# Start of a gated linear attention and MLP kernel: the order of constants, and the queue and place of three loads

## The chip, the cores and the metric

The kernel runs on one core of a Trainium2 chip. A core has a matrix engine (TensorE, PE in the profile), a vector engine (VectorE, DVE), an engine for activation functions and copies (ScalarE, ACT), a general engine (GpSimd, POOL) and one that mainly issues transfers (SyncE, SP). They run side by side, each through its own list of instructions in order, and wait for one another on semaphores. Transfers between the large memory (HBM) and the core's own memory (SBUF) are issued by SP or ACT on hardware queues, or by POOL on a software queue, which can also convert types on the way. PSUM is the small memory that TensorE writes to.

The metric is the device time in microseconds, as a median over runs.

## What is computed

The inputs are q, k, v and alpha, each of 4 batches, 8 heads, 768 positions and head size 48, and two weight matrices. Per head a 48 x 48 state decays by alpha and takes in an outer product; the result goes through a two-layer network with a gelu.

```python
for t in range(S):
    state = alpha[:, :, t, :, None] * state + np.einsum('bhd,bhe->bhde', k[:, :, t], v[:, :, t])
    y[:, :, t] = np.einsum('bhd,bhde->bhe', q[:, :, t], state)
# x: y with the heads side by side, 3072 x 384
h = x @ w_in                                       # 384 x 2048
g = 0.5 * h * (1.0 + np.tanh(c * (h + 0.044715 * h * h * h)))
return g @ w_out                                   # 2048 x 384
```

All comes and goes in float32; the kernel works in bfloat16 and float16 inside.

## The kernel before

The sequence is cut into six chunks of 128 positions, and two batches at a time form a pair: twelve pairs, worked through as (chunk 0, batches 0 and 1), (chunk 0, batches 2 and 3), (chunk 1, ...) and so on. They are called pair 0, pair 1, pair 2 below; `j` is the batch within a pair.

For each pair ScalarE takes the logarithm of alpha (L296 or L298), TensorE sums it along the positions with a triangular matrix (L283 and L287, or L315 and L317), and ScalarE forms exp of the sums: `b`, `binv` and `bend` (L332, L338). VectorE multiplies q by `b` and k by `binv` (L349: `qp`, `kp`). TensorE transposes both (L359), ScalarE or VectorE copies the transposes out of PSUM (L377: `qkT`), TensorE forms the scores of a batch (L414: `at`) and VectorE masks them (L421: `atm`). Then `y` is the product of the masked scores with v (L463), plus the state's part from the second chunk on (L460). `y` is copied (L470: `x`), transposed (L477) and copied again (L481: `xT`). The state is carried on with L431 and L448 (for the first pairs after k has been transposed back, L385 and L392).

The network runs in twelve blocks, one a pair: layer 1 in 16 column blocks of three matmuls each (L487: `hT`), a gelu for each (L493), and layer 2 (L501: `acc`). The result is copied (L508) and stored (L513). ScalarE loads its function table anew when it goes from exp and logarithm to gelu or back (L208).

Pairs 0 and 1 are "packed". Their q, k and alpha come in four pieces each, of 32 partitions with 192 values in a run, so that a run is long; the positions of a chunk then lie in another order, and the sums of L283 need special block masks, `ut_blk` and `blk`, in place of the plain triangle.

What is issued in what order on every engine is decided when the program is built. `tasks` makes a list of tasks with costs, dependencies and priorities; `Scheduler.order` goes through it with costs from the table `W` and gives each engine its list. Where it sees TensorE idle for long in the first 60 us by its own plan, it puts in filler matmuls on a tile of zeros (L217), whose results nobody reads. The number of fillers ahead of the first real matmul is the planned idle time divided by `cold`. The orders of the constants and of the loads are not planned; they are written out:

- `run` (from L728) has the constants: `zero`, `ones`, the triangle and the identity (these two in part on POOL), then the zeros in the pads of the ring buffers for `la`, `qp` and `kp` (L738), the zero states (L741), then `blk` and `ut_blk` (L742 to L750), then a bfloat16 copy of the triangle (L751). Except for the two parts on POOL, all of that is VectorE's.
- `RINGS` lists the packed pieces (tensor, pair, piece) and the engine that issues each. SP or ACT issue them from the first instruction on.
- `LOADS` lists what POOL's software queue loads: `v0` is v of pair 0 (converted to bfloat16 on the way), `in 0` a quarter of w_in, `out 0` a quarter of w_out, a bare number all of a later pair. `gatek0` is not a load: POOL copies one column of k of pair 0 into a scratch tile (L250), and so does not go on before that k has landed. A step beginning with `p` loads the four pieces of a packed tensor on POOL's queue; there was none.

POOL's list at the start is therefore: gate on k of pair 0, v of pair 0, gate on q of pair 1, w_in 0, v of pair 1, w_in 1 to 3, w_out 0 and 1, then pair 2. Loads on a queue take eight semaphores in turn, so a load also waits until the one eight places ahead of it has landed.

## Time and profile before

| | |
|---|---|
| median of 5 runs | 188.19 us (187.1 to 189.17) |
| the profiled execution | 186.78 us |
| its span, first to last instruction | 185.0 us |
| PE busy | 174.7 us, 94% |
| ACT busy | 136.2 us, 74% |
| DVE busy | 105.2 us, 57% |
| granted TensorE clock | 1.0 |

The profile is one execution. The page gives each engine's busy time, then the span in 40 slices with the busy share of each in tenths, the transfers, the chain of work that ended last, and the costliest groups of instructions. The trace behind it gives single instructions, what they waited for, and when a transfer landed. Times within the span count from its first instruction. A busy PE counts fillers too: there are 16 of them, 7.9 us in sum.

Some transfers at the start, from the trace:

| load | queue | issued | landed |
|---|---|---|---|
| q, pair 0, four pieces | SP and ACT | 1.66 to 2.16 | 5.00 to 5.80 |
| k, pair 0, four pieces | SP | 3.40 to 4.71 | 6.03 to 7.38 |
| alpha, pair 1, four pieces | SP | 5.20 to 6.61 | 7.70 to 9.37 |
| q, pair 1, four pieces | SP | 7.08 to 8.51 | 9.96 to 11.12 |
| v, pair 0 | POOL | 8.08 | 14.67 |
| k, pair 1, four pieces | SP | 8.98 to 10.44 | 12.53 to 15.03 |
| w_in, part 0 | POOL | 11.73 | 16.62 |
| v, pair 1 | POOL | 12.47 | 18.80 |
| w_in, parts 1, 2, 3 | POOL | 13.66, 14.39, 15.15 | 21.01, 23.21, 25.12 |
| w_out, part 0 | POOL | 15.90 | 27.11 |

### The profile page before, as it was taken

The numbers are of one execution on the slowest core, as the hardware profiler recorded it, in microseconds if no ns is written. First come the engines' busy times: TensorE is split into PE (matmuls) and PEld (weight loads), VectorE is DVE, ScalarE is ACT, GpSimd is POOL, SyncE is SP. The second block draws the span as 40 slices with busy tenths as digits, with TensorE's granted clock in tenths as the row PEclk, the third lists the DMA queues.
The fourth block names the chain that finished last, engine by engine and source line by source line (L and its number), as shares of the span: only waits on it lengthen the run. The fifth ranks groups of instructions, "written<-read, shape, count | busy, mean of one in ns | idle before, by whom it ended". The sixth has DMA issues, their size and how long they took to land.

```text
span 185.0 us, 4590 instructions
## 1 busy us (share of the span) xinstructions
PE 174.7 (94%) x1840; PEld 127.4 (69%) x1842; DVE 105.2 (57%) x235; ACT 136.2 (74%) x308; POOL 58.6 (32%) x64
## 2 busy tenths in 40 slices
PE   7595999999999999999999999999999999999992
PEld 2353779666687787687688769667677677686861
DVE  8576763079677596597499798596644715000000
ACT  3495869865979869859799759788789884491931
POOL 2259545994663566565660200000000000000000
PEclk9999999999999999999999999999999999999999
DMA  5899999999999999999999976054171290311102
GB/s 159 220 175 175 184 211 204 211 226 172 185 276 190 157 234 198 178 231 202 180 216 231 186 198 119 19 130 99 24 168 53 43 200 4 87 43 46 43 0 85
DMA packets 50613, 27.56 MB, mean 149 GB/s; under 512 B 37984, under 2 KB 47712, under 8 KB 50592
## 3 DMA queue, kind: packets, MB, share of 16 engines
q0 software_dynamic: 31904, 17.30, 68.7%
q1 hardware_dynamic: 18112, 9.57, 20.7%
q10 hardware_dynamic: 576, 0.39, 0.7%
q8 instruction: 14, 0.23, 0.6%
q14 instruction: 7, 0.06, 0.1%
HBM read 25.17 MB, written 4.72 MB: 162 GB/s over the span
## 4 chain that ended last, share of the span: by engine, by line
PE 81%; DMA 8%; ACT 4%; DVE 3%; issue 1%; SPq 1%; POOL 0%; POOLq 0%; DVEq 0%
PE acc L501 32%; PE hT L487 31%; PE at L414 4%; DMA v<-in_v_dram 4%; PE qkT_ps L359 3%; PE yps L463 3%; PE yps L460 2%; PE cum L315 2%; PE kv L431 2%; DMA qkT<-kp 2%; PE xT_ps L477 2%; DMA k<-in_k_dram 1%; DMA a<-in_alpha_dram 1%; DVE atm L421 1%; DVE st L448 1%
## 5 line engine op out<-in xcount | busy, mean ns | idle before, releaser
L493 ACT ACTIVATE gT<-hT 128x256 bf16<-128x256 f32 x192 | 63.9, 386 | 10.6 <-PE hT L487 9.9
L487 PE MATMUL hT<-xT,w_in 128*128 128x256 bf16 x576 | 70.5, 273 | 0.3 <-ACT gT L493 0.2
L501 PE MATMUL acc<-w_out,gT 128*128 128x384 bf16 x384 | 68.9, 326 | 0.0
L487 PEld LDWEIGHTS <-w_in 128*128 128x128 bf16 x576 | 54.0, 98 | 8.6 <-DVE xT L481 0.6
L501 PEld LDWEIGHTS <-gT 128*128 128x128 bf16 x384 | 35.6, 97 | 20.3
L421 DVE TENSOR_TENSOR atm<-at,ut 128x512 bf16<-128x512 f32 x48 | 31.1, 686 | 14.5 <-PE at L414 13.8
L349 DVE TENSOR_TENSOR qp<-q,b 128x768 bf16<-128x768 f32 (+1 forms) x15 | 11.8, 793 | 15.4 <-ACT b L338 15.4
L508 ACT COPY ot<-acc 128x384 f32<-128x384 f32 x16 | 7.7, 480 | 14.3 <-PE acc L501 13.3
L230 POOL DMA_DIRECT2D v<-in_v_dram x13 | 14.6, 1123 | 10.3 <-DMA v<-in_v_dram 2.6
L338 ACT ACTIVATE b<-cum 128x768 bf16<-128x768 f32 (+1 forms) x15 | 10.2, 683 | 7.5 <-PE cum L317 2.6
L230 POOL DMA_DIRECT2D k<-in_k_dram x11 | 12.2, 1108 | 10.3 <-DVE kp L349 4.7
L230 POOL DMA_DIRECT2D a<-in_alpha_dram x11 | 12.2, 1113 | 7.0 <-DMA q<-in_q_dram 2.8
L230 POOL DMA_DIRECT2D q<-in_q_dram x11 | 12.2, 1111 | 6.3 <-DMA w_out<-in_moe_w_out_dram 1.1
L208 ACT ACT_TABLE_LOAD x9 | 11.5, 1283 | 2.8 <-issue 2.6
L448 DVE TENSOR_TENSOR st<-stmp,bend 64x192 bf16<-64x192 f32 x32 | 11.3, 353 | 1.6
L349 DVE TENSOR_TENSOR kp<-k,binv 128x768 bf16<-128x768 f32 (+1 forms) x15 | 11.8, 792 | 0.4 <-ACT binv L338 0.2
L446 DVE TENSOR_TENSOR stmp<-kv,st 64x192 f32<-64x192 f32 x32 | 11.3, 352 | 0.9 <-PE kv L431 0.6
L493 ACT ACT_TABLE_LOAD x9 | 11.5, 1283 | 0.2
L470 ACT CAST x<-yps 128x384 bf16<-128x384 f32 x13 | 6.2, 479 | 6.8 <-PE yps L463 6.8
L470 DVE CAST x<-yps 128x384 bf16<-128x384 f32 x11 | 6.1, 556 | 7.7 <-PE yps L463 7.6
L463 PE MATMUL yps<-v,atm 128*128 128x48 bf16 x192 | 8.7, 183 | 1.6 <-DMA v<-in_v_dram 0.9
L338 ACT ACTIVATE binv<-cum 128x768 bf16<-128x768 f32 (+1 forms) x15 | 10.2, 679 | 0.0
(61 smaller groups left out, 161.8 us busy)
## 6 DMA issues: line engine op xcount, KB each, us to landing
out_dram<-ot SPq DMA_DIRECT2D x24, 192.0 KB, 2.7
a<-in_alpha_dram POOLq DMA_DIRECT2D x9, 384.0 KB, 13.1
q<-in_q_dram POOLq DMA_DIRECT2D x9, 384.0 KB, 13.2
k<-in_k_dram POOLq DMA_DIRECT2D x9, 384.0 KB, 13.4
v<-in_v_dram POOLq DMA_DIRECT2D x11, 192.0 KB, 12.9
w_in<-in_moe_w_in_dram POOLq DMA_DIRECT2D x4, 384.0 KB, 8.1
w_out<-in_moe_w_out_dram POOLq DMA_DIRECT2D x4, 384.0 KB, 11.3
k<-in_k_dram SPq DMA_DIRECT2D x8, 96.0 KB, 3.3
```

The costliest lines, as they stand in the source:

```text
L208: nc.scalar.add_instruction(mybir.InstLoadActFuncSet(name=nc.get_next_instruction_name(), act_func_set_id=i, engine=mybir.EngineType.Activ ...
L230: (nc.sync if e == "SP" else nc.gpsimd).dma_start(u[n][:, lo:hi].rearrange("t b h d -> t (b h) d"), src)
L338: self.nc.scalar.activation(u[n].rearrange("t i h d -> t i (h d)")[:, lo:hi], cum, AF.Exp, scale=1.0 if n == "b" else -1.0)
L349: self.nc.vector.tensor_tensor(out, rows, b, op=ALU.mult)
L421: self.nc.vector.tensor_tensor(u["atm", i][:, o], u["at", i][:, o], self.ut[:, None, :].to_broadcast([self.C, self.H // 2, self.C]), op=AL ...
L446: nc.vector.tensor_tensor(s[ps], acc, old[ps, :, fs], op=ALU.add)
L448: nc.vector.tensor_tensor(new[ps, :, fs], acc, u["bend"][ps, i, :, None].to_broadcast([64, H // 2, D]), op=ALU.mult)
L463: nc.tensor.matmul(y[:, h, :], u["atm", i][:, h % 2, h // 2, :], u["v"][:, i, h, :], start=c == 0, stop=True, skip_group_check=True)
L470: self.copy(e)(x, u["y", i].rearrange("t h d -> t (h d)"))
L487: self.nc.tensor.matmul(h, self.w_in[:, j, nt * self.C:(nt + 1) * self.C], self.xT[c][:, j, lo:hi].rearrange("p g t -> p (g t)"), start=j ...
L493: return lambda e: self.nc.scalar.activation(self.gT[c % self.NG][:, nt, lo * self.C:hi * self.C], f.pop(("h", c, lo, nt)), AF.Gelu_apprx_ ...
L501: self.nc.tensor.matmul(f["acc", c, b], self.gT[c % self.NG][:, nt, b * self.C:(b + 1) * self.C], self.w_out[:, nt, :], start=nt == 0, sto ...
```

## The change

In `run`, the zeros in the ring buffers' pads and the zero states move behind the block masks. In `LOADS`, POOL waits for q of pair 0 instead of k of pair 0, and has no second gate; k of pair 1 is loaded by POOL, in the same four pieces, right behind v of pair 0, and its four entries leave SP's list; v of pair 1 comes behind w_in 0 and w_in 1. In the planner's table `cold` goes from 400 to 380.

```diff
-    ... piece=330, piece_issue=450, begin=2700, cast_p=2300, ln_packed=1040, cold=400, fill=216, zero=1100,
+    ... piece=330, piece_issue=450, begin=2700, cast_p=2300, ln_packed=1040, cold=380, fill=216, zero=1100,
...
-    LOADS = ('gatek0', 'v0', 'gateq1', 'in 0', 'v1', 'in 1', 'in 2', 'in 3', 'out 0', 'out 1', '2a', ...)
+    LOADS = ('gateq0', 'v0', 'pk1', 'in 0', 'in 1', 'v1', 'in 2', 'in 3', 'out 0', 'out 1', '2a', ...)
...
-    RINGS = (... ('q', 1, 3, 'SP'), ('k', 1, 0, 'SP'), ('k', 1, 1, 'SP'), ('k', 1, 2, 'SP'), ('k', 1, 3, 'SP'))
+    RINGS = (... ('q', 1, 3, 'SP'))
...
         make_identity(nc, self.ident)
-        for i in range(max(self.BUFS[n] for n in self.ring)):
-            for n in self.ring:
-                if i < self.BUFS[n]:
-                    nc.vector.memset(self.ring[n][i][:, :, :, self.D:64], 0.0)
-        for b in range(self.B):
-            for i in range(2):
-                nc.vector.memset(self.state[b][i], 0.0)
         nc.vector.memset(self.blk, 0.0)
...
             nc.vector.tensor_copy(self.ut_blk[0][a:b, a + 1:b], self.ut_h[a:b, a:b - 1])
+        for i in range(max(self.BUFS[n] for n in self.ring)):
+            for n in self.ring:
+                if i < self.BUFS[n]:
+                    nc.vector.memset(self.ring[n][i][:, :, :, self.D:64], 0.0)
+        for b in range(self.B):
+            for i in range(2):
+                nc.vector.memset(self.state[b][i], 0.0)
         nc.vector.tensor_copy(self.ut, self.ut_h)
```

Because the planner works with the dependencies of the new loads, the built program also differs in the order of instructions. TensorE has nine fillers ahead of the first sum instead of eight. On VectorE the masks of pair 0's second batch come ahead of the second of pair 1's `qp`, and that `qp` behind both of pair 1's `kp`. On ScalarE one of pair 1's four `qkT` copies comes behind the first gelu instead of ahead of the table load. On TensorE the transposes of pair 1's q and k, the first `y` and the first `xT` stand in another order, and layer 1 of the first block is cut into groups of other sizes. From pair 2 on the orders on PE, ACT and DVE are as before.

## The prediction

> **What bounds the kernel now.** I read the page's busy slices first, to see where TensorE is not full.

> ```profile
> PE   7595999999999999999999999999999999999992
> PEld 2353779666687787687688769667677677686861
> DVE  8576763079677596597499798596644715000000
> ACT  3495869865979869859799759788789884491931
> ```

> A slice is 4.6 us. PE is at 9 from the fifth slice on, until the last output. So the time is a start of some 19 us, then a stream of matrix work that does not stop. A change at the start is worth what it moves the beginning of that stream, if nothing the stream reads then comes late.

> Next the chain that ended last, in order of time (start, length, what):

> ```profile
> 0.74 2.64 DMA a<-in_alpha_dram
> ...
> 4.71 2.67 DMA k<-in_k_dram
> 7.54 0.19 POOL gate L250
> 7.72 0.36 issue
> 8.08 6.59 DMA v<-in_v_dram
> 14.71 0.37 PE yps L463 x8
> 15.11 0.48 ACT x L470
> ```

> The first output `y` waits for v of pair 0; that was issued at 8.08, because POOL's gate waited for the last piece of k. It took 6.59 us. The waits between 0 and 35 us (total, times, longest) tell what else was late:

> ```profile
> POOL gate L250 <- DMA k<-in_k_dram: 5.7, 1, 5.7
> ...
> PEld L283 <- DVE ut_blk L749: 2.0, 1, 2.0
> ...
> PE yps L463 <- DMA v<-in_v_dram: 0.9, 1, 0.9
> ```

> PE's first real work, the decay sums at 5.85, waited for the block masks; the logarithm it reads was done at 5.21. And v cost PE only 0.9: had it been there, the masks of pair 0 would have let `y` start near 13.8. Last, the timeline, where the stream begins:

> ```profile
> 19.62 1.28 ACT L493 ACT_TABLE_LOAD   x1
> 20.91 2.60 ACT L493 ACTIVATE gT<-hT 128x256 bf16<-128x256 f32 x8
> 23.83 0.37 PE L463 MATMUL yps<-v,atm 128*128 128x48 bf16 x8
> 24.04 0.81 PE L487 MATMUL hT<-xT,w_in 128*128 128x256 bf16 x6
> ```

> First gelu at 20.91, ninth column block of layer 1 at 24.04, after pair 1's first `y`. From there PE has no gap worth naming, so 24.04 is my marker.

> **Part 1: masks ahead of the other constants.** Nothing is added. The 11 pad memsets and 8 state memsets (1.12 to 4.30) go behind blk, ut_blk and their copies (4.30 to 5.87, 1.57 us). The masks are then done near 2.7, the pads near 4.3, the states near 5.9, the cast of ut near 6.1; each still lies ahead of its first reader (qp near 7.3). The first logarithm ends at 4.8, but the plan puts a ninth filler matmul (0.43) behind the eight that began at 1.19, so PE is free at 5.08. Sums start at 5.08, not 5.85: 0.77 earlier. The first b, qp and kp follow by the same 0.77: kp at 7.78, and k of pair 0 landed at 7.38, so its cover holds by 0.4.

> **Part 2: the gate on q.** The last piece of q landed at 5.80, k's at 7.38. By the same steps as before (0.16 to the gate, 0.19 for it, 0.36 issue), v goes out at 6.50, 1.58 earlier. Its packets began 2.08 after the issue (10.16), so now 8.58. Before, 3.24 us passed from the first to the last packet, because k of pair 1 ran beside it on SP's queue; between 10.16 and 14.9 that queue moved 0.42 MB in 4.74 us, against 0.64 MB in the three microseconds from 5 to 8. From 8.58 the neighbour is q of pair 1 (issued 7.08 to 8.94), which stands to v as k stood before: its first piece landed 1.38 after 8.58, where k's would have landed 1.4 after 10.16. So I move the whole collision 1.58 forward: v lands at 13.1 instead of 14.67, and q's last piece at 13.2 to 13.4 instead of 11.12. That is the price of this part, and qp of pair 1 pays it.

> **Part 3: k of pair 1 on POOL's queue.** SP loses four issues of 0.45; nothing is behind them until the first store at 45.99, so that is worth nothing. POOL gains four. No row shows this piece there; the nearest, the first layer's weights, took 0.75 an issue, so at most 3.0 us, at least 4 x 0.45 by SP's row. POOL is through with them by 10.8, before v's packets end at 11.8: hidden, either way. [...] The row: v's issue at 8.08 lay beside four scaling products of VectorE and took 1.28, against 1.15 to 1.18 later. [...]

> k's bytes (0.39 MB) then follow v's. Rates bound them: 0.215 MB/us on SP's queue alone gives 1.8; the contended 0.089 for the first 0.9 us adds some 0.4. Packets end at 14.0, and with 0.7 to land (the lag behind the packets of the first weight part) k is there at 14.7 (14.1 to 15.5; before 15.03). Its first use, behind the second output's masks on VectorE, comes at 15.6. [...] Were only SP's issue time at stake, this part would be worth 0; the halved rate above says the same, and my sum counts no bandwidth, only an earlier start.

> **Part 4: v of pair 1 behind two weight parts.** Order now: v, k, two parts of w_in, v, two parts. Weights land 2.0 apart (23.21, 25.12, 27.11), and v's packets took 1.3. From 13.9: parts at 16.7 and 18.9, v at 20.8 (was 18.80), parts three and four at 22.5 and 24.5 (were 23.21 and 25.12, so 0.6 to 0.7 earlier). POOL reuses a semaphore eight loads back; part three now waits for v of pair 0 (13.1), still with six loads queued ahead, so no starvation. `y` of pair 1 takes v at 23.0 at the earliest: covered by 2.2 us. If that cover went, PE would stand at `y` with layer 1 behind it, one for one.

> **The sum.** Step by step on the new order. Scores of the first output at 10.95 (was 11.59), masked by 12.7; y at 13.15 (was 14.71). VectorE comes to qp of pair 1 at 12.7, waits for q until 13.35 and holds the second output's masks behind it: these end at 15.2, hardly before the old 15.44. Second y 15.25 (was 17.18; PE no longer sits behind transposes), its copy at 15.75. VectorE then does xT, two kp and a qp to 17.15 and the second xT to 17.5. Layer 1 starts at 17.9 (was 19.12). ScalarE's last copy before the table load ends at 18.2; first gelu 19.5 (was 20.91), 1.4 earlier. Then the new order gives half of it back: one qkT copy (0.59) now stands behind the first gelu and waits for transposes that need a PSUM buffer freed by VectorE's state update near 19.7. It ends at 20.9; scores 20.9, masks to 22.6 (was 23.45), the pair's other scores, y at 23.0, marker at 23.2 to 23.4: 0.65 to 0.85 before 24.04. Parts three and four are there in time. After the marker all orders are the same but for groups of three matmuls; the later loads (second half of pair 2's alpha, landed 36.00 and used at 37.05) move by 0.6 too, so none turns late. Gain 0.8. The profiled execution took 186.78 (span 185.0) and would take 186.0; it was 1.4 faster than the median of the runs, 188.19, and the same 0.8 off that gives **187.4**.

> **Rivals.**
> - *q is not delayed.* If software packets take less of the engines than they did from k, q lands near 12.3, VectorE does not wait, second masks end at 14.6 and the first gelu is at 19.0. The next late thing is part three and four of w_in: with 22.5 against 24.04 and 24.5 against 25.81 they cap the gain at 1.3 to 1.5. 186.8. For it: 10.39 to 11.12, where q's tail was not slowed by v's beginning. Against: the halved rate after it.
> - *Slower: k lands late in the software queue.* Place: VectorE's kp of pair 1, with the second xT behind it, so layer 1 as well. Each microsecond past 15.6 is lost one for one; the gain of 0.8 is gone at 16.4, and 1.9 is lost at 18.3. A piece fills only 32 partitions, and four sit between v and the weights; if they moved at the contended 0.089 MB/us to the end, k lands at 16.9: 188.7. [...] Nothing in the trace shows four such pieces on this queue.
> - *Nothing comes of it.* Masks and v move, but the marker hangs on the qkT copy behind the first gelu; if ScalarE does it after further waits it eats the rest: 188.1.

> **Chances.** My sum 0.52, q in time 0.18, nothing 0.15, k late 0.15. Medians here wander by about 0.5, and 1% (1.9 us) is about what a measurement of this kernel can tell from no change. Over 1% faster needs q in time and more, with a kind draw; slower needs the far half of the k case. Range 186.0 to 189.0: from the q case with its spread up to the milder k case.

> **What would show it.** Right: sums at about 5.1; v issued near 6.5 and landed near 13.1; q of pair 1 after 13; k before 15.6; first gelu near 19.5; marker near 23.3; no wait on w_in over 0.3. Wrong: kp waiting for a DMA, v landing before 12, a PE gap at `y` of pair 1, or a stall after 30 us that the trace of before lacks.

## The result and the profile after

The changed kernel took 187.5 us (median of 36 runs, 185.84 to 189.28), the kernel before 187.89 (71 runs, 186.67 to 189.8). The ratio is 0.9979 with a 95% interval of 0.9963 to 0.9995: 0.2% faster, 0.4 us. The forecast was 187.4, by a gain of 0.8.

The median hides different kinds of execution. The mean granted TensorE clock that each one reports tells two of them apart. In 12 of the 36 the clock was full (1.0, in one 0.996); their median is 186.33. In 24 it was lowered for a while (mean 0.991); their median is 187.85. The 71 executions of the kernel before come without a clock, but they too fall into two groups: 34 up to 187.51, with a median of 187.09, and 37 from 187.77 on, with 188.17. In the later comparisons the kernel before had its clock lowered in 26 of 181 executions only. So against the faster group of before the change gains some 0.75 us where its clock is full, and in two executions of three it loses more than that again.

The profiled execution of the changed kernel is one of the latter: 188.37 us, span 186.6. The busy slices of its page, with the granted clock:

```profile
PE   7785999999999999999999999999999999999992
...
DVE  7657584059767687487489798696653715000000
...
PEclk9997899999999999999999999999999999999999
```

Slices four and five (14.0 to 23.3 us) have a clock of 0.7 and 0.8. Before, every slice had 9:

```profile
PEclk9999999999999999999999999999999999999999
```

VectorE has 5 in the third slice (9.3 to 14.0 us), where it had 7. What the engines waited for, from the waits between 10 and 26 us (total, times, longest):

```profile
ACT qkT L377 <- PE qkT_ps L359: 2.9, 3, 1.5
...
DVE qp L349 <- DMA q<-in_q_dram: 1.7, 1, 1.7
...
PE qkT_ps L359 <- DVE qp L349: 1.6, 1, 1.6
```

And the timeline, with the first sums ahead of it:

```profile
5.10 1.44 PE L283 MATMUL cum<-la,ut_blk 128*128 128x384 f16 x7
...
6.48 0.82 PE L283 MATMUL cum<-la,ut_blk 128*128 128x384 f16 x7
...
7.41 0.49 ACT L338 ACTIVATE b<-cum 128x384 bf16<-128x384 f32 x1 [1.95 <-PE cum L287]
...
13.73 0.40 PE L414 MATMUL at<-qkT 64*128 64x128 bf16 x8
...
14.05 0.37 PE L463 MATMUL yps<-v,atm 128*128 128x48 bf16 x8
...
15.37 0.56 DVE L349 TENSOR_TENSOR qp<-q,b 128x384 bf16<-128x384 f32 x1 [1.71 <-DMA q<-in_q_dram]
...
15.99 0.40 PE L359 MATMUL qkT_ps<-ident,qp 128*128 128x128 bf16 x4 [1.56 <-DVE qp L349]
...
17.92 0.61 PE L359 MATMUL qkT_ps<-ident,kp 128*128 128x128 bf16 x4
```

The first `y` starts at 14.05, 0.66 earlier than in the profile of before. The gate and the wait for v, which stood in the chain there, are no longer what TensorE waits for: v landed at 13.87, 0.2 behind the masks, while TensorE was still at the second scores. The wait has moved to q of pair 1. Its last piece landed at 15.25 (before: 11.12), VectorE held `qp` for it by 1.71 us with two masks behind, and TensorE stood for 1.56. At 17.92 the same four transposes that took 0.40 take 0.61. The windows say why (length, then busy time of each engine with counts, granted clock, DMA share, GB/s):

```profile
6.40:16.64 10.24, 6.78 (x89) 4.49 (x89) 5.30 (x10) 6.73 (x19) 8.81 (x13) 1.00 1.23 204
16.64:20.05 3.41, 2.99 (x24) 1.99 (x25) 2.52 (x6) 1.43 (x3) 3.19 (x4) 0.50 1.85 181
20.05:25.00 4.95, 4.73 (x54) 3.29 (x53) 3.56 (x8) 4.74 (x11) 2.29 (x3) 1.00 1.27 205
```

From 16.64 to 20.05, 3.41 us, the clock is at half. The trace's own record of the clock begins with full clock at 6.40, three times 3.41 us ahead of 16.64; all views count the time ahead of the record as full. But the first seven sums, at 5.10, took 1.44 us where the next seven, behind 6.40, took 0.82. Before, the record began at 4.40, ahead of the sums:

```profile
5.85 0.83 PE L283 MATMUL cum<-la,ut_blk 128*128 128x384 f16 x7 [1.19 <-DVE ut_blk L749]
```

So in this profile the sums begin 0.75 earlier than before, and the first `b` that follows them only 0.14 earlier (7.41 against 7.55). The first gelu is at 22.06 (20.91 before) and the marker, the ninth column block of layer 1, at 25.55 (24.04).

Landing times of the loads, in this profile and before: v of pair 0 13.87 (14.67), k of pair 1 15.81 (15.03), w_in 0 to 3 16.95, 18.87, 22.15, 24.07 (16.62, 21.01, 23.21, 25.12), v of pair 1 20.24 (18.80).

### The profile page after: what moved, and what is told of

Read it like the earlier page. It is cut to its first block, busy times and chain, and to the rows that moved or that the text cites. A ratio compares the mean times of both kernels' runs of the same rounds, so it can differ in the third digit from the quotient of the medians.

```text
span 186.6 us, 4594 instructions
## 1 busy us (share of the span) xinstructions
PE 177.0 (95%) x1843; PEld 129.1 (69%) x1845; DVE 105.3 (56%) x235; ACT 136.2 (73%) x308; POOL 60.5 (32%) x67
## 4 chain that ended last, share of the span: by engine, by line
PE 72%; DMA 18%; ACT 3%; POOL 2%; issue 2%; DVE 1%; ACTq 1%; SPq 0%; POOLq 0%
PE acc L501 31%; PE hT L487 26%; DMA v<-in_v_dram 8%; DMA w_out<-in_moe_w_out_dram 6%; PE at L414 3%; PE qkT_ps L359 3%; DMA q<-in_q_dram 2%; PE yps L460 2%; PE yps L463 2%; PE cum L315 2%; DMA qkT<-kp 2%; PE kv L431 2%; PE xT_ps L477 1%; POOL w_in L257 1%; ACTq L242 1%
## 5 line engine op out<-in xcount | busy, mean ns | idle before, releaser
L493 ACT ACTIVATE gT<-hT 128x256 bf16<-128x256 f32 x192 | 63.7, 386 | 10.4 <-PE hT L487 9.6
L487 PE MATMUL hT<-xT,w_in 128*128 128x256 bf16 x576 | 70.7, 273 | 0.3 <-ACT gT L493 0.2
L487 PEld LDWEIGHTS <-w_in 128*128 128x128 bf16 x576 | 53.9, 98 | 8.6 <-DVE xT L481 0.6
L501 PEld LDWEIGHTS <-gT 128*128 128x128 bf16 x384 | 35.6, 97 | 20.2
L349 DVE TENSOR_TENSOR qp<-q,b 128x768 bf16<-128x768 f32 (+1 forms) x15 | 11.9, 793 | 16.8 <-ACT b L338 13.4
L508 ACT COPY ot<-acc 128x384 f32<-128x384 f32 x16 | 7.7, 480 | 14.3 <-PE acc L501 13.3
L230 POOL DMA_DIRECT2D v<-in_v_dram x13 | 14.6, 1120 | 10.1 <-PE xT_ps L477 3.8
L349 DVE TENSOR_TENSOR kp<-k,binv 128x768 bf16<-128x768 f32 (+1 forms) x15 | 11.8, 792 | 0.4 <-ACT binv L338 0.2
L377 ACT COPY qkT<-qkT_ps 128x512 bf16<-128x512 bf16 (+1 forms) x10 | 7.1, 726 | 4.9 <-PE qkT_ps L359 4.7
L470 ACT CAST x<-yps 128x384 bf16<-128x384 f32 x13 | 6.2, 478 | 6.0 <-PE yps L463 6.0
L470 DVE CAST x<-yps 128x384 bf16<-128x384 f32 x11 | 6.1, 556 | 7.3 <-PE yps L463 7.3
## 6 DMA issues: line engine op xcount, KB each, us to landing
q<-in_q_dram POOLq DMA_DIRECT2D x9, 384.0 KB, 13.1
k<-in_k_dram POOLq DMA_DIRECT2D x9, 384.0 KB, 13.2
v<-in_v_dram POOLq DMA_DIRECT2D x11, 192.0 KB, 13.2
```

Of the source, the lines that this page charges most:

```text
L230: (nc.sync if e == "SP" else nc.gpsimd).dma_start(u[n][:, lo:hi].rearrange("t b h d -> t (b h) d"), src)
L349: self.nc.vector.tensor_tensor(out, rows, b, op=ALU.mult)
L470: self.copy(e)(x, u["y", i].rearrange("t h d -> t (h d)"))
L487: self.nc.tensor.matmul(h, self.w_in[:, j, nt * self.C:(nt + 1) * self.C], self.xT[c][:, j, lo:hi].rearrange("p g t -> p (g t)"), start=j ...
L493: return lambda e: self.nc.scalar.activation(self.gT[c % self.NG][:, nt, lo * self.C:hi * self.C], f.pop(("h", c, lo, nt)), AF.Gelu_apprx_ ...
L501: self.nc.tensor.matmul(f["acc", c, b], self.gT[c % self.NG][:, nt, b * self.C:(b + 1) * self.C], self.w_out[:, nt, :], start=nt == 0, sto ...
```

## The experiments

Theory A, formed on this profile: v's early packets share the transfer engines with q of pair 1, q comes late (its pieces landed 4.5 us after their issue, as a median; 2.8 before), VectorE and TensorE stand, and the clock is halved for 3.4 us. Between two changes of the clock the record of this profile has 10.24, 3.41 and 167.25 us and that of before 180.91: 3, 1, 49 and 53 times 3.413 us. One such stretch is called a window below. The theory supposes, and these two records alone do not show, that how busy TensorE was decides the clock of a window, and that the windows lie differently in each execution. Its main rival, B: the masks in front are what gains, the loads bring nothing or harm. A third, C, came with the two groups of times that the kernel before shows, near 187.1 and 188.2.

All kernels compute the whole result. Ratios are against the kernel before on the same chip in the same hour. "Lowered" counts the executions whose mean clock was under 0.995; one window at half clock makes it 0.991. A mean of 0.996 to 0.999 is not counted: in e9's profile (0.997) the clock fell at 184.38, behind the last matmul.

| run | ratio (95%) | median, us | lowered |
|---|---|---|---|
| changed kernel | 0.9979 (0.9963 to 0.9995) | 187.50 | 24 of 36 |
| e1 masks only | 0.9993 (0.9965 to 1.0021) | 187.54 | 4 of 12 |
| e2 late gate | 0.9966 (0.9942 to 0.9990) | 186.60 | 1 of 13 |
| e3 changed, fillers in the gap | 0.9966 (0.9944 to 0.9988) | 186.88 | 0 of 12 |
| e4 before, fillers in the gap | 1.0045 (1.0003 to 1.0087) | 188.26 | 0 of 5 |
| e5 loads only | 0.9967 (0.9943 to 0.9990) | 187.01 | 0 of 20 |
| e6 early gate only, masks in front | 1.0073 (1.0046 to 1.0099) | 188.46 | 8 of 20 |
| e7 before, eleven fillers | 0.9996 (0.9965 to 1.0028) | 187.28 | 4 of 12 |
| e8 late gate, fillers in the gap | 0.9975 (0.9953 to 0.9998) | 186.96 | 2 of 20 |
| e9 late gate, old constants, eleven fillers | 0.9957 (0.9937 to 0.9977) | 186.77 | 0 of 22 |
| e10 changed, v of pair 1 one part earlier | 0.9964 (0.9941 to 0.9987) | 186.92 | 10 of 20 |
| e11 loads only, eleven fillers | 0.9935 (0.9913 to 0.9958) | 186.26 | 0 of 12 |
| e12 before again | 0.9991 (0.9966 to 1.0017) | 187.05 | 2 of 18 |

### e1: the masks alone

The changed kernel with `LOADS` and `RINGS` of before:

```diff
-    LOADS = ('gateq0', 'v0', 'pk1', 'in 0', 'in 1', 'v1', 'in 2', ...)
+    LOADS = ('gatek0', 'v0', 'gateq1', 'in 0', 'v1', 'in 1', 'in 2', ...)
-    RINGS = (... ('q', 1, 3, 'SP'))
+    RINGS = (... ('q', 1, 3, 'SP'), ('k', 1, 0, 'SP'), ('k', 1, 1, 'SP'), ('k', 1, 2, 'SP'), ('k', 1, 3, 'SP'))
```

> The constants in the new order and nine fillers, with the loads and queues of before. Theory A (in the changed kernel v's early packets halve the rate of q of pair 1, q lands late, VectorE and with it TensorE stand, and the TensorE clock is lowered): here q lands at about 11.1 us as before, v at 14.7, and TensorE's first sums at 5.1 instead of 5.85 are spent at the wait for v; time 0.0 to 0.3 us under before. Theory B (the masks are what the changed kernel gains by, the loads bring nothing): 0.4 us or more under before.

The first sums start at 4.94 and the marker is at 24.07, where it was. The waits between 10 and 26 us show where the lead went:

```profile
PE yps L463 <- DMA v<-in_v_dram: 1.8, 1, 1.8
```

It was 0.9 before. TensorE comes to that wait 0.4 us earlier (13.40 against 13.77), and v landed 0.5 later in this profile (15.13). Theory B's gain of 0.4 does not show in the profile; the interval of the times, 0.7 us faster to 0.4 slower, would still allow it.

### e2: the late gate

```diff
-    LOADS = ('gateq0', 'v0', 'pk1', ...
+    LOADS = ('gatek0', 'v0', 'pk1', ...
```

The planner then gives the old order on PE, DVE and ACT, so this run changes that order too and not the gate alone.

> The changed kernel with POOL's gate back on k of pair 0, so that v goes out near 8.0 us instead of 6.5 to 7.0; k of pair 1 stays on POOL's queue. The planner then gives back the old order on TensorE, VectorE and ScalarE. Theory A: v meets only q's tail and no k, so q of pair 1 lands at 11.1 to 11.6, v no later than in the changed kernel (12.8 to 13.6), k near 14.5; no stand of over 1 us at q's product; faster than the changed kernel by 0.5 to 1.2 us, so 0.9 to 1.6 under before. Theory B, or a rival by which the early gate is what gains: v late again, time as before or slower than the changed kernel by 0.3 to 0.8.

q of pair 1 landed at 11.23 and the clock was lowered in one execution of 13. The ratio went from 0.9979 to 0.9966; the intervals overlap, and 0.6 us under before is less than the 0.9 to 1.6 that I expected. v landed at 13.93, no earlier than in the changed kernel's profile (13.87) and not at 12.8 to 13.6. In this trace v's packets start from 10.36 to 12.92, in the changed kernel's from 9.15 to 12.92. This pair overstates it: in the six profiles with the early gate they start at 8.81 to 9.15 and the last at 12.66 to 12.97, in the three with the late gate and k on POOL's queue (e2, e8, e9) at 10.28 to 10.55 and 12.92 to 13.53. So a start some 1.4 us earlier bought an end some 0.4 earlier, and q paid for it: A's first half holds (the early gate makes q late), but my figure for v did not.

### e3 and e4: fillers where TensorE stood

```diff
         for t in order:
             ...
             t.emit(t.engine)
+            if t is self.first_y:
+                self.fill(6)(t.engine)
```

`first_y` is the `y` task of pair 0's first batch. e3 has this on the changed kernel, e4 on the kernel before.

> The changed kernel with six more filler matmuls of 512 columns (1.3 us at full clock) on TensorE right behind the first y, where it stood idle for 1.56 us. No work is left out. Theory A, second half (the idle stretch lowers the clock for 3.4 us in the executions where a window of the clock's watch falls on it, and that costs 1.1 to 1.3 us each time): mean granted clock 1.0 in nearly all executions instead of 0.991 in about two thirds, median 186.3 to 186.7 against 187.5. If the lowered clock has another cause, or costs nothing because the work there waits anyway: clock as often 0.991, time 187.5 or up to 0.5 more.

> The kernel before with the same six fillers behind its first y. If the executions of before fall into two groups near 187.1 and 188.2 for the same reason, the lowered clock, its median goes from 187.9 to about 187.2 to 187.6 (the fillers lie on the path here, at most 1.3 us, less what TensorE waits for the copy of x anyway). If the two groups have another cause: 188.0 to 189.

e3: no execution of 12 had a lowered clock, and the median was 186.88 where the changed kernel had 187.50. The same stretch in its profile:

```profile
13.57 0.56 DVE L349 TENSOR_TENSOR qp<-q,b 128x384 bf16<-128x384 f32 x1 [0.87 <-DMA q<-in_q_dram]
13.63 0.36 PE L463 MATMUL yps<-v,atm 128*128 128x48 bf16 x8 [0.47 <-DMA v<-in_v_dram]
13.84 1.46 PE L217 MATMUL idle<-zero 128*128 128x512 bf16 x6
```

q came at 13.45 here, so the fillers even stood in the way by about 1 us (transposes at 15.13, `qp` done at 14.13). The six fillers are all that differs from the changed kernel, and the count of lowered executions went from 24 of 36 to none of 12: that the idle stretch there takes part in lowering the clock is shown. That it gains time is not. The median is 0.6 lower, but before's was 0.6 lower too in that hour (187.30 against 187.89), and the intervals of the two ratios overlap. Against the changed kernel's full-clock executions (186.33) 0.5 is left, which the fillers in the way may cost. The marker is at 23.50, and the first sums ran at full speed: seven took 0.82 from 4.95, with full clock from 4.89.

e4 missed. At full clock in all five, it was yet 0.45% slower, at 188.26, against an expected 187.2 to 187.6. In its profile the sums ran slowly:

```profile
5.85 1.46 PE L283 MATMUL cum<-la,ut_blk 128*128 128x384 f16 x7 [1.06 <-DVE ut_blk L751]
7.26 1.44 PE L283 MATMUL cum<-la,ut_blk 128*128 128x384 f16 x7
```

In the profile of before each set of seven took 0.83. Here the clock record begins with full clock at 9.60; before, at 4.40. The eight fillers had run from 1.2 to 4.8, then TensorE stood for 1.06 us. Part of e4's loss is that late clock, part its fillers, which stand in the way of the transposes; one profile does not divide the two. It led to theory C: the upper group of before's times comes from a clock that is granted in full one window of 3.4 us late, because TensorE stands between the fillers and the sums.

### e5: the loads alone

The kernel before with `LOADS` and `RINGS` of the changed one (the reverse of e1's diff); constants and `cold` as before.

> The loads and queues of the changed kernel with the constants in the order of before and eight fillers. If the masks in front are worth something in the changed kernel, by the 0.77 us that the first sums come earlier or by TensorE having no idle stretch between fillers and sums: 187.8 to 188.8, with lowered clock in half or more of the executions, and a first full clock late in some. If the loads alone make the changed kernel (masks worth nothing there, since q of pair 1 is what VectorE waits for): same as the changed kernel, 187.3 to 187.7.

This went against what I expected: 187.01, and no lowered clock in 20 executions. The loads alone are no worse than the whole change. The timeline has the same wait for q, but shorter:

```profile
13.93 0.36 PE L463 MATMUL yps<-v,atm 128*128 128x48 bf16 x8 [0.15 <-DMA v<-in_v_dram]
14.13 0.56 DVE L349 TENSOR_TENSOR qp<-q,b 128x384 bf16<-128x384 f32 x1 [0.82 <-DMA q<-in_q_dram]
...
14.75 0.40 PE L359 MATMUL qkT_ps<-ident,qp 128*128 128x128 bf16 x4 [0.47 <-DVE qp L349]
```

q landed at 14.01, 1.2 earlier than in the changed kernel's profile with the same loads; that is why the stand is shorter here (TensorE's began at 14.28, there at 14.43). The marker, 23.52, is where e3 has it with the masks in front (23.50). e3's fillers stood in the way, though, so this pair does not price the masks; e11 below does it better. Four of the 20 executions stand at 187.92 to 188.16 although their mean clock is full, as part of before's do and none of the changed kernel's.

### e6: the early gate without k on POOL's queue

e1's kernel with one word changed:

```diff
-    LOADS = ('gatek0', 'v0', 'gateq1', ...
+    LOADS = ('gateq0', 'v0', 'gateq1', ...
```

> The constants in the new order; of the loads only POOL's first gate is changed, to q of pair 0. k of pair 1 stays on SP behind q, and v of pair 1 where it was. Theory A (v's packets beside q's halve q's rate, whichever queue k is on): v issued near 6.6, landed 13 to 14, q of pair 1 at 13.3 or later, k of pair 1 at 15.5 to 16.5; POOL's second gate holds the weights until q is there, so w_in part 0 comes near 18.5; time 187.5 to 188.5, slower than the masks alone by up to 1. Rival (k's four pieces behind v on POOL's queue are what delays q in the changed kernel): q at 11.1 to 12.0 and v at 13, faster than the masks alone by 0.5 to 1, so near 186.5.

q landed at 13.54 with k on SP's queue, so it is v's packets that delay q, not k's pieces behind v; the rival's 11.1 to 12.0 is out. v landed at 13.70. The kernel lost 0.7%, at the waits for the weights that POOL's second gate held back:

```profile
POOL gate L250 <- DMA q<-in_q_dram: 10.0, 2, 5.6
...
PEld L487 <- DMA w_in<-in_moe_w_in_dram: 2.6, 2, 1.6
```

w_in 0 was issued at 14.20 (10.46 in the changed kernel), since the second gate waits for the very q that the first one makes late. With k on POOL's queue the kernel needs no such gate, and e5, without it, gains where e6 loses. The early gate with k on SP's queue and no second gate was not run, so the place of k and the missing gate are not told apart.

### e7: eleven fillers in front of the first sum

```diff
-    ... cold=400, ...
+    ... cold=320, ...
```

This alone, on the kernel before, leads to eleven fillers instead of eight; nothing else in the built program differs.

> The kernel before with eleven fillers ahead of the first sum instead of eight, so that TensorE is busy without a break from 1.2 to 5.9 us; nothing else differs. Theory C (the upper group of before's executions, near 188.2, comes from a clock that is granted in full one window of 3.4 us later, because TensorE stands from 4.65 to 5.85): upper group gone or much thinner, median 187.0 to 187.3 on a chip where before shows both groups. If the groups have another cause: as before, or 0.1 later, since eleven cold fillers end at 5.88.

Half of C holds. Of the 8 executions with full mean clock none was above 187.45, and their median was 186.94; beside them 21 of before's 56 such executions were above 187.6. But 4 of 12 had a lowered clock, more than before's share (7 of 63), and the gain in the median is within the noise (0.9996). Both kinds together are 4 of 12 here and 28 of 63 there, so fewer disturbed executions are not shown. The profile is one of these four: full clock from 7.09, half from 17.33 for 3.41 us, again three windows later.

### e8 and e9: the late gate with fillers

e8 is e2 with four fillers behind the first `y`. e9 is e5 with the gate on k of pair 0 and `cold=320`.

> The late gate (k of pair 1 on POOL's queue, gate on k of pair 0, masks in front) with four fillers behind the first y, 0.87 us, where TensorE waits 0.5 to 0.7 us for copies anyway. With the late gate one execution of 13 had a lowered clock. If the fillers only guard the clock: 186.4 to 186.7, no lowered clock. If they stand in the way of the transposes behind them: 0.2 to 0.5 slower than the late gate alone.

> The constants of before, eleven fillers ahead of the first sum, POOL's gate on k of pair 0, and k of pair 1 on POOL's queue behind v. It joins what the runs so far speak for: TensorE busy from 1.2 to 5.9 us, q of pair 1 undisturbed, v with no k beside it, and no early arrival at the wait for v. If these add: clock lowered or late in few executions, median 186.3 to 186.8, 0.6 to 1.0 under before. If the masks in front carry part of what the late gate gained: 186.9 to 187.3.

e8: 186.96, lowered in two of 20; nothing gained over e2 (186.60), perhaps something lost, as the second reading had it; the ratios, 0.9975 and 0.9966, have overlapping intervals. Its profile shows why fillers behind the first `y` are no guard here. TensorE stood ahead of `y`, as v came at 14.96, and the clock was halved from 15.27:

```profile
15.00 0.36 PE L463 MATMUL yps<-v,atm 128*128 128x48 bf16 x8 [1.79 <-DMA v<-in_v_dram]
```

With the masks in front TensorE came to that wait at 13.21, in the profile of before at 13.77.

e9: 186.77 with no lowered clock in 22, and none above 187.57. That is in the range expected, at its upper end.

### e10: the place of v of pair 1

```diff
-    ... 'in 0', 'in 1', 'v1', 'in 2', ...
+    ... 'in 0', 'v1', 'in 1', 'in 2', ...
```

> The changed kernel with v of pair 1 behind one part of w_in, as before, instead of two. By the prediction v of pair 1 has 2 us in hand, so its place is worth nothing by itself: time as the changed kernel within 0.4, v near 18.5, part 1 of w_in near 20.2, parts 2 and 3 unmoved. If the place matters: 0.5 or more away from the changed kernel, with a TensorE gap at layer 1's fifth column block.

v of pair 1 landed at 18.36, w_in 1 at 20.30, parts 2 and 3 at 22.21 and 24.07, as in the changed kernel. Full-clock executions had 186.11 (186.33 there), lowered ones 187.47 (187.85), in shares of 10 and 10. 0.2 to 0.4 apart, within the 0.4 expected: the place is worth little or nothing.

### e11: loads only, eleven fillers

e5 with `cold=320`.

> The loads of the changed kernel, the constants of before, eleven fillers. In the run with eight fillers and these loads (187.0) no clock was lowered, but some executions stood near 188. If those are executions whose clock came one window late, the fillers remove them: 186.3 to 186.9. If the stand at q of pair 1 is what makes them: as with eight fillers, or with lowered clocks and near 187.5 as in the changed kernel.

186.26 us, 0.9935 (0.9913 to 0.9958): the best of all. All twelve executions lie between 185.68 and 186.63. The windows that were shown of the changed kernel:

```profile
6.40:16.64 10.24, 7.78 (x103) 5.03 (x101) 6.61 (x13) 7.40 (x20) 8.64 (x13) 1.00 1.20 201
16.64:20.05 3.41, 3.33 (x39) 2.47 (x39) 2.34 (x7) 2.61 (x5) 2.37 (x3) 1.00 1.81 184
20.05:25.00 4.95, 4.73 (x63) 3.52 (x64) 3.82 (x8) 4.22 (x13) 2.52 (x3) 1.00 1.29 202
```

TensorE is busy 7.78 of the first 10.24 us, where the changed kernel had 6.78, and the second window has full clock. q landed at 13.94, the wait cost VectorE 0.75, and:

```profile
14.68 0.40 PE L359 MATMUL qkT_ps<-ident,qp 128*128 128x128 bf16 x4 [0.35 <-DVE qp L349]
...
18.70 1.28 ACT L493 ACT_TABLE_LOAD   x1
```

First gelu 20.00, marker 23.45. Its median equals that of the changed kernel's full-clock executions (186.33) within 0.1: with eleven fillers in its place, the whole gain of the change is here without its first part. Beside e9 it also says that the early gate as such is no harm once TensorE does not stand long: with the late gate w_in 2 landed at 23.52, here at 23.25, and e9's median is 0.5 higher; the intervals overlap, so this is a hint and no more.

### e12: before again

> The kernel before, for one more profile. If its executions near 188.2 have a clock that is full only at 7.8 to 9.7 us or is lowered for 3.4 us after 14 us, and those near 187.1 have neither, one of the two is seen here with the time that goes with it.

This profile had neither the late nor the lowered clock (full from 4.97, 186.71 us) and so shows only the lower group. That the upper group of before has the late clock is therefore not seen directly. It rests on e4's profile and on counts of the executions with full mean clock: none of 42 with eleven fillers (e7, e9, e11) was above 187.6, against 48 of 139 of the kernel before beside them. With the same loads on both sides it is none of 8 against 21 of 56 (e7 and before) and none of 12 against 4 of 20 (e11 and e5). I take it as likely, not as shown.

## Why the prediction was right, and where it was not

**The marker and the full-clock time.** I put the marker 0.65 to 0.85 ahead of 24.04 and the gain at 0.8. The early-gate profiles with full clock and the same orders of work (e3, e5, e11) have it at 23.50, 23.52 and 23.45, 0.5 to 0.6 ahead, and the changed kernel's full-clock executions are some 0.75 below before's faster group. The sum came out near, but by errors that cancelled, as the parts show.

**Part 1, masks in front.** The sums start at 5.10; I had 5.08. In the changed kernel's profile the step behind that failed: the first seven sums ran before the full clock and took 1.44, so `b` came 0.14 earlier and not 0.77. Where the clock was full in time, as in e3, the step held (scores at 10.98; I had 10.95), and the lead then ended at v, or with the early gate at q of pair 1. I had seen VectorE wait there for 0.65, and did not ask what was left of Part 1 behind it; e11, with the masks behind and eleven fillers, is as fast. I charged nothing for the part. e1 and e8 show that TensorE comes earlier to the wait for v and stands there longer (1.77 and 1.79; 0.94 before), in part because v came 0.3 to 0.5 later.

**Part 2, the gate.** Moving the collision as a whole was the right picture: q suffers, and v gains less than its earlier start. The sizes were too kind. The gate came when q of pair 0 was in, at 5.99 to 6.21 in these profiles and not 5.80, and v went out at 6.77 to 6.99 instead of 6.50. I had v's packets last 3.24 us; with the stragglers, the trace of before has 3.81 (10.16 to 13.97). So v landed at 13.54 to 13.93 over six early-gate profiles, not 13.1, and q at 13.45 to 15.25, not 13.2 to 13.4. The stand at `qp` was 1.7 us in the changed kernel's profile, where I had 0.65.

**Part 3, k on POOL's queue.** Its four issues took 0.55 each (2.2 us in sum; I had 1.8 to 3.0) and lay ahead of v's last packets. They ran from 8.27 to 10.46, in part beside VectorE's products, and v's issue took 1.28 again, so the row was right. (The issue in the profile of before lay beside three products, not four.) No run shows VectorE's work holding POOL's issues up by more than the 0.1 us between this 1.28 and the 1.15 to 1.18 of the row; the far half of the k rival would need more. k's four issues, beside three products from 8.41 to 10.11 and behind them, took 0.55 to 0.57 each. k landed at 15.81, above my 14.7 and even the 15.5 of its range, but later work hid it: its first use came at 17.31. I gave the missing second gate no term; e6 shows that with the early gate it costs much.

**Part 4, v of pair 1.** Landed at 20.24 (20.8 forecast), w_in 2 and 3 at 22.15 and 24.07 (22.5 and 24.5), no wait on either; e10 confirms that the place itself carries nothing.

**Half given back behind the first gelu.** I had the first gelu 1.4 ahead and some 0.6 of it given back. In e3 the first gelu was 0.86 ahead of before and the marker 0.54, but at the first matmul of layer 2 (32.74 against 33.57 before) the lead was 0.83 again; e5 and e11 have 0.8 there too. So the lead was smaller than I thought, because q was later, and hardly any of it was given back: two errors that cancel.

**Behind the marker.** I let the lead run to the end. It did not: in e5 0.66 of its 0.80 was left at the last copy, and 0.41 at the end of the span. The last copies, before and in e5:

```profile
181.73 0.48 ACT ot L508
...
181.07 0.48 ACT ot L508
```

The first 0.15 goes where TensorE waits for transposes by DMA near 152 us, 0.17 before and 0.33 in e5; why is open. The 0.25 at the end is a price of Part 3, which I put at nothing. At the end SP waits for its eight semaphores, always in the same order, about 0.06 us for each on which all has landed. SP issues 60 transfers before and 56 with k on POOL's queue. As they take the semaphores in turn, the last store has the eighth before and the fourth now, so four waits that used to pass while the store was on its way come behind it. SP's wait for that store, before and in e5:

```profile
SPq L782 <- DMA out_dram<-ot: 1.0, 1, 1.0
...
SPq L782 <- DMA out_dram<-ot: 1.3, 1, 1.3
```

From the last matmul to the end it takes 3.29 to 3.32 us in the six profiles with k on SP's queue, and 3.54 to 3.56 in the eight with k on POOL's.

By these profiles the gain would be 0.4, by the medians of the groups 0.75; a single profile of each kernel does not decide between them.

**What was not in the sum: the clock.** It was full in every slice of before's profile, and I listed no case in which it is not. With it, a gain of 0.75 between the faster groups became 0.4 between the medians. None of the three rivals was this one. "q is not delayed" fell: q was later than forecast. k was late, but not late enough for anyone to wait. "Nothing comes of it" fell with the marker at full clock. That the median came so near the forecast, 187.5 against 187.4, is luck: I took the gain off 188.19, the median of five runs of before; against the 187.89 of the 71 runs the same gain would have given 187.1, and the clock made up the difference.

## What to carry to other kernels

An engine that reaches a wait earlier has gained nothing (in e1 TensorE came to the wait for v 0.4 us earlier, and the marker stayed). It may lose, where its idle time grows and its clock falls with that, as in the changed kernel's executions with a lowered clock (187.85 against 186.33); so work ahead of a wait should be moved only together with what ends the wait. A transfer put out earlier can take its share from those already on the way, as v did here (its packets ended some 0.4 us earlier, q's last piece landed 2.3 to 4.1 later); look for the reader of each of those, not only of the one moved. And look at the spread of the single runs with the granted clock of each before a median is explained: groups 1.5 and 1.1 us apart, in other shares before and after, gave a difference of 0.4 that no group has. And at the end of a kernel look at the order in which transfers are waited for.

## What the runs showed of the hardware that I had not expected

```profile
13.30:16.71 3.41, 2.15 (x37) 1.43 (x35) 2.79 (x6) 1.86 (x5) 2.89 (x4) 1.00 1.71 177
16.71:20.12 3.41, 3.41 (x24) 2.49 (x22) 1.33 (x4) 2.17 (x3) 2.83 (x4) 0.50 1.36 195
...
4.97:8.38 3.41, 1.91 (x23) 1.38 (x23) 1.36 (x10) 1.14 (x4) 0.18 (x1) 1.00 0.77 222
8.38:11.80 3.42, 2.90 (x37) 2.00 (x37) 2.44 (x5) 3.36 (x11) 1.41 (x2) 1.00 1.13 196
```

- The changed kernel's executions with a lowered clock were 1.5 us slower than its others (187.85 against 186.33). Not all of that need be the halved clock: in both profiles of such executions with these loads and the masks in front (changed kernel, e10) the first sums were slow as well.
- v's packets, begun some 1.4 us earlier on the software queue, ended some 0.4 earlier when q's packets were beside them; q's last piece came 2.3 to 4.1 us later for it than in before's profile.
- The first full clock came between 4.19 and 9.60 us from the start, in kernels that all begin with matmuls at 1.2.
